# Four early expert tiles instead of two, three places for weights, and buffers of their own for the experts' squares

## The chip, the cores and the metric

One NeuronCore of one Trainium2 chip runs the whole program; the other cores are idle. The metric is the device time of one execution in microseconds. Beside it a profile gives, for one execution, every instruction's start and duration on the engines TensorE (PE, its weight loads as PEld), VectorE (DVE), ScalarE (ACT), GpSimd (POOL) and the queue engine SyncE (SP), and the clock that TensorE was granted.

## The reference

Three layers stand in a chain. Each token comes out of the first as one row of 512 numbers (8 heads of 64); there are 4 x 768 = 3072 tokens.

```python
# 1. retention: a decaying state per batch element and head
state = gamma * state + einsum('bhd,bhe->bhde', k[:, :, t], v[:, :, t])
y[:, :, t] = scale * einsum('bhd,bhde->bhe', q[:, :, t], state)
# 2. dense layer with a leaky activation: 512 -> 2048 -> 512
h = x @ w_in
x2 = (maximum(h, 0) + alpha * minimum(h, 0)) @ w_out
# 3. eight experts, each token goes to the one with the largest logit
expert_idx = argmax(normed(x2) @ normed(expert_emb).T / tau, axis=1)
out[mask] = gate_w[mask, None] * (maximum(x2[mask] @ w1[e], 0) @ w2[e])   # 512 -> 1024 -> 512
```

## The kernel before, in words

**Precision.** Every large product is taken in fp16 with both operands split into a high and a low half: high x high, high x low and low x high, three matmuls for one, summed in PSUM.

**Blocks.** The 3072 tokens are 24 tiles of 128, in 6 blocks of 4 tiles. For each block the retention makes the rows, and the dense layer runs as 16 steps: `mm1` gives 128 of the 2048 hidden columns for all 512 tokens of the block (12 matmuls with 512 columns), ScalarE and VectorE apply the activation and split the result, and `mm2` (four tiles of 3 matmuls) adds them into four accumulators. Of the last block the four tiles' `mm2` run with delays of 0, 2, 4 and 5 steps, so that its tiles end one after the other.

**Routing.** When a tile's accumulator is full, `Route` squares it, splits it into a payload of 514 words (512 values as two fp16 halves, gate weight, token number), transposes the payload by DMA on the SP queue, multiplies it with the experts' embeddings, takes the largest logit, and finds the row in a DRAM table where the token goes: expert e owns rows 3072 e and on, in the order of arrival. POOL scatters the payload there by an indirect DMA. Blocks 0 to 4 are routed a block at a time; the last block tile by tile, since everything behind it waits for it.

**The experts' weights.** From the second block on (about 200 to 650 us) the 8 experts' weights are split to fp16 halves and written to the DRAM buffer `wsplit`, in 16 halves of four pieces. `half_scale` (L729) squares the four raw pieces on ScalarE, for the sum that sets the scale; the squares themselves are thrown away, into a corner of one of the output buffers (`out_ring.bufs[g % 2]`). TensorE adds the sums over the partitions (`total`). Then `half_pair` (L739) splits each piece into the next of the two output buffers of `out_ring` (ScalarE writes the high half, VectorE the low half), SP writes it to `wsplit` (512 KB) and loads a further raw piece. Raw pieces and output buffers are parts of one 32 KB buffer per partition, `stage`.

**Experts' tiles.** A tile is 128 rows of the table of one expert: POOL gathers the rows by an indirect DMA, SP transposes them by DMA, `mm1e` (96 matmuls with 128 columns) and `mm2e` (24 matmuls with 512 columns) run on TensorE, VectorE scales the result, and POOL scatters it to the output. Which expert a tile belongs to is computed in the kernel: even tiles take the experts from the first up, odd tiles from the last down. Tile t's weights (`load_w`, four pieces of 1 MB, L1177) are fetched only where the expert changes, into `win16` for even tiles and `wout16` for odd ones, the places of the dense layer's weights, as these come free.

**Early tiles.** After block 4, `pick` (L851) takes the expert with the most tokens so far and gathers its first two tiles (t = -2 and -1), whose rows are in the table already. Their weights go to `stage`. These two tiles give TensorE work while the last block is routed. All other tiles (0 to 21 always, up to 7 more under a condition) follow when the counts of all tokens are known.

**Order.** The program is recorded and then ordered by a planner (`Plan.issue`, L252): it simulates engines and DMAs with fixed costs, takes at each step the instruction that can start first (a matmul only 1500 ns after what it waits for on another engine), and writes each engine's instructions in that order. On the chip each engine runs its own list strictly in order, and so does the SP queue. Since every instruction is recorded through one helper, nearly all rows of the trace carry its line, L146; a row is told apart by the buffers it names. Buffer names in the trace: `stage<-stage` on ScalarE is a square of `half_scale`, `stage<-stage,se` a split of `half_pair`; `wsplit<-stage` the write; `acce` the sums; `hat_buf` the early tiles' columns, `qk_buf` their payloads; `f_buf` in the experts' part the gathered payloads; `xT` there the columns and results.

Of the kernel before, what the change touches and what calls it, by code (L numbers as in the profile page):

```python
# [26 lines left out]
BW = BT * P  # L27
KD = DM // P
KF = DFF // P
NPRE = 2  # L30
NMIN = NTILE - NPRE
NSLOT = NMIN + E - 1
SL = 30
# [14 lines left out]
_n = 0  # L48
for _name, _w in (
    ("ks", NCH * H), ("w8", E), ("base8", E), ("first", E * E),  # L50
    ("tau0", SL), ("odd", SL), ("tidx", SL), ("p", 1), ("prow", NPRE), ("ones", P), ("tok", NTILE),
):
    _COLS[_name] = (_n, _n + _w)
    _n += _w
# [3 lines left out]
def _constants():  # L58
    gamma = 1.0 - 2.0 ** (-5.0 - np.arange(H))
    p = np.arange(P)  # L60
    c32 = np.zeros((P, NCOL), np.float64)

    def put(name, a):
        lo, hi = _COLS[name]
        c32[:, lo:hi] = np.broadcast_to(np.asarray(a, np.float64).reshape(-1, hi - lo), (P, hi - lo))

    c = np.arange(NCH)
    put("ks", gamma[None, None, :] ** -(P * c[None, :, None] + p[:, None, None] + 1.0))
    e = np.arange(E)
# [8 lines left out]
    put("prow", E * CAP + P * np.arange(NPRE)[None, :] + p[:, None])  # L78
# [247 lines left out]
def retention_prelu_moe_kernel(ctx: ExitStack, tc, qkv, w_in, w_out, alpha, emb, tau, w1, w2,  # L326
# [14 lines left out]
    def buf(name, shape, dt=F32):  # L341
        return sbuf.tile([P, *shape], dt, name=name, tag=name)
# [102 lines left out]
    def square_sum(src, acc, junk):  # L445
        A.activation(out=junk, in_=src, func=AF.Square, accum_out=acc)
# [268 lines left out]
    iwe = [buf(f"iwe{g}", [E]) for g in range(2)]  # L715
    HALVES = [(e, which) for e in range(E - 1, -1, -1) for which in range(2)]
    raw_ring = Ring([stage[:, 2 * k:2 * k + 2, :].rearrange("p c x -> p (c x)") for k in range(6)])
    out_ring = Ring([stage16[:, 2 * k:2 * k + 2] for k in (6, 7)])
    half_t = {}

    def half_load(p):
# [7 lines left out]
    def half_scale(n):  # L729
        e, which = HALVES[n]  # L730
        acc = tmp("acce", [4])
        for g in range(4):
            square_sum(half_t[n, g], acc[:, g:g + 1], out_ring.bufs[g % 2][:, :, 0, :])
        s = tmp("se", [1])
        c = (C_W1, C_WIDE)[which]
        pow2_inverse(pow2(total(acc, 4), s, c), iwe[which][:, e:e + 1], c)
        half_t[n] = s
# [108 lines left out]
    sel, m8 = buf("sel", [E]), buf("m8", [1])  # L846
    pre_idx = buf("pre_idx", [2], I32)
    pre_e = buf("pre_e", [1], I32)
    pre_row, first_row, first_other = buf("pre_row", [1]), buf("first_row", [1]), buf("first_other", [1])

    def pick():  # L851
        ps = m_ring.next()
        T.matmul(out=ps[:, 0:E], lhsT=ones16, rhs=csum, start=True, stop=True)
        m = tmp("pm", [1], n=1)
        V.tensor_reduce(out=m, in_=ps[:, 0:E], axis=AX.X, op=ALU.max)
        w = tmp("pw", [E], n=1)
        V.scalar_tensor_tensor(out=w, in0=ps[:, 0:E], scalar=m, in1=col("w8"), op0=ALU.is_equal, op1=ALU.mult)
        V.tensor_reduce(out=m8, in_=w, axis=AX.X, op=ALU.max)
        V.tensor_scalar(out=sel, in0=w, scalar1=m8, scalar2=None, op0=ALU.is_equal)
        V.tensor_scalar(out=pre_e, in0=m8, scalar1=-1.0, scalar2=float(E), op0=ALU.mult, op1=ALU.add)  # L860
        row = tmp("prow", [1], n=1)
        V.tensor_scalar(out=row, in0=m8, scalar1=-float(CAP), scalar2=None, op0=ALU.mult)
        V.tensor_scalar(out=pre_idx, in0=col("prow"), scalar1=row, scalar2=None, op0=ALU.add)
        V.tensor_tensor(out=pre_row, in0=col("prow")[:, 0:1], in1=row, op=ALU.add)
        V.scalar_tensor_tensor(out=first_row, in0=sel[:, 0:1], scalar=float(NPRE * P), in1=col("p"),
                               op0=ALU.mult, op1=ALU.add)
        V.tensor_tensor(out=first_other, in0=pre_row, in1=first_row, op=ALU.subtract)

# [38 lines left out]


    PRE = range(-NPRE, 0)
    wbuf = (win16, wout16, stage16)  # L910

    def cutter(buf_):
        words, at_ = buf_, [0]
# [23 lines left out]
        return [Ring([view(cut(n)) for _ in range(k)]) for view, n, k in parts]  # L937

    PAY, XT, H2 = (as_pay, PW), (as_xt, 512), (as_h2, 1024)
    pre_pay, = carve(qk_buf, (*PAY, NPRE))  # L940
    pre_xt, = carve(hat_buf, (*XT, NPRE))
    pre_h2, = carve(vp_buf, (*H2, NPRE))
    gather_ring, = carve(f64_buf, (*PAY, 6))
    xt_ring, = carve(xT[NB % 2], (*XT, 3))
    y_ring, = carve(xT[(NB - 1) % 2], (lambda a: a, DM, 4))
    h2_ring = Ring(carve(st_bd, (*H2, 2))[0].bufs + carve(x2T_buf, (*H2, 1))[0].bufs)
    opt_xt, opt_pay = carve(stage, (*XT, NSLOT - NMIN), (*PAY, NSLOT - NMIN))
    gt, x2T, h2, slot_idx = {}, {}, {}, []

    def gather(t):  # L950
# [126 lines left out]
    def sl(shape, dt=F32):  # L1077
# [3 lines left out]
        if dt != F32:  # L1081
# [17 lines left out]

    ntl = sl([E])  # L1100
    V.tensor_scalar(out=ntl, in0=ci, scalar1=1, scalar2=None, op0=ALU.max)
    V.scalar_tensor_tensor(out=ntl, in0=sel, scalar=-float(NPRE), in1=ntl, op0=ALU.mult, op1=ALU.add)

    t8 = sl([E, E])
    V.tensor_tensor(out=t8, in0=col("first").rearrange("p (a b) -> p a b", a=E),
# [9 lines left out]
    prod = sl([SL, E - 1])  # L1115
    wts = sl([2, E - 1])
    dsel = sl([E - 1])
    V.tensor_tensor(out=dsel, in0=sel[:, 1:E], in1=sel[:, 0:E - 1], op=ALU.subtract)
    V.tensor_scalar(out=wts[:, 0, :], in0=ntl[:, 0:E - 1], scalar1=-float(P), scalar2=float(CAP),
                    op0=ALU.mult, op1=ALU.add)  # L1120
    V.scalar_tensor_tensor(out=wts[:, 0, :], in0=dsel, scalar=float(NPRE * P), in1=wts[:, 0, :], op0=ALU.mult, op1=ALU.add)
# [38 lines left out]

    iw12 = sl([E])
    V.tensor_tensor(out=iw12, in0=iwe[0], in1=iwe[1], op=ALU.mult)
    pre_w = buf("pre_w", [1])
    ew = sl([E])
    V.tensor_tensor(out=ew, in0=iw12, in1=sel, op=ALU.mult)
    V.tensor_reduce(out=pre_w, in_=ew, axis=AX.X, op=ALU.add)
    wsl = sl([SL])
    for e in range(E):
        eq = tmp("eq", [SL])
# [7 lines left out]
    def load_w(t):  # L1177

        for piece in range(4):
            which, o = divmod(piece, 2)  # L1180
            dst = wbuf[t % 2 if t >= 0 else 2][:, 4 * piece:4 * piece + 4].rearrange("p c a x -> p (c a x)")
# [5 lines left out]
            which_e = pre_e[0:1, 0:1] if t < 0 else ctl[0:1, 0, t:t + 1]  # L1187
# [12 lines left out]
    def mm1e(t):  # L1200
        xt = x2T.pop(t)
        w = wbuf[t % 2 if t >= 0 else 2]
        h = h2[t] = (pre_h2 if t < 0 else h2_ring).next()
        for q in range(2):
            ps = x_ring.next()
            with plan.unit("PE"):
# [14 lines left out]
    def mm2e(t):  # L1221
        h = h2.pop(t)
        g = gt.pop(t)
        w = wbuf[t % 2 if t >= 0 else 2]
        ps = h_ring.next()
        for q in range(2):
            with plan.unit("PE"):
# [5 lines left out]
        if t >= 0:  # L1233
# [2 lines left out]
                                   op0=ALU.mult, op1=ALU.add)  # L1236
        y = y_ring.next()
        V.tensor_scalar(out=y, in0=ps, scalar1=g.bitcast(F32)[:, DM:DM + 1],
                        scalar2=wsl[:, t:t + 1] if t >= 0 else pre_w, op0=ALU.mult, op1=ALU.mult)
# [93 lines left out]
```

## Time and profile before

| | before |
|---|---|
| median of three runs | 1017.08 us (1011.92 to 1018.13) |
| profiled execution | 1014.34 us, span 1012.6 us |
| TensorE busy | 929.1 us (92%) |
| VectorE busy | 569.1 us (56%) |
| ScalarE busy | 466.2 us (46%) |
| GpSimd busy | 93.3 us (9%) |
| mean granted clock of TensorE | 0.967 |

The span reaches from the first to the last instruction; the execution is a little longer. Busy TensorE time counts matmuls as if they had their full length, so that at the low clock it is busy for longer with the same work. A wait in the trace is the idle time of an engine just before an instruction, with what ended it.

### The profile page before, as it was taken

How to read it: one execution, taken by the hardware profiler on the slowest of the kernel's cores; microseconds unless marked ns; L12 is line 12 of the kernel's file. 1: busy time of each engine (PE TensorE's matmuls, PEld its weight loads, DVE VectorE, ACT ScalarE, POOL GpSimd, SP SyncE). 2: the span in 40 equal slices, each digit the busy share in tenths (PEclk: the TensorE clock that was granted, in tenths of full speed). 3: DMA queues.
4: the chain of work that ended last, by engine and by line, in shares of the span. 5: the costliest groups of instructions: out<-in, count | busy, mean ns of one | idle time of the engine just before them, and what ended most of it. 6: DMA issues, size and time to landing. Idle time of an engine off the chain costs nothing. (4 is left out here: it accounts for less than half of the span.)

```text
span 1012.6 us, 18929 instructions
## 1 busy us (share of the span) xinstructions
PE 929.1 (92%) x7100; PEld 558.5 (55%) x7100; DVE 569.1 (56%) x1477; ACT 466.2 (46%) x825; POOL 93.3 (9%) x110
## 2 busy tenths in 40 slices
PE   5797889999998999999999899999599999988995
PEld 5774555555544544444444344446476776765763
DVE  4889988488766866686556448638422221221231
ACT  2568865385767777686565557322011010110100
POOL 0000000000100020001000200111311211232010
PEclk9798879999999999999999999999799999999998
DMA  8988623547789866766676655687564599634760
GB/s 298 303 255 268 221 97 112 177 115 196 253 231 231 201 228 221 218 209 209 197 208 187 209 166 161 237 322 176 136 194 115 141 308 319 174 95 114 165 269 23
DMA packets 129823, 201.44 MB, mean 199 GB/s; under 512 B 89726, under 2 KB 90110, under 8 KB 124608
## 3 DMA queue, kind: packets, MB, share of 16 engines
q1 hardware_dynamic: 123168, 179.42, 59.8%
q0 software_dynamic: 6560, 20.77, 6.0%
q8 instruction: 57, 0.93, 0.4%
q14 instruction: 38, 0.31, 0.1%
HBM read 204.59 MB, written 51.14 MB: 253 GB/s over the span
## 5 line engine op out<-in xcount | busy, mean ns | idle before, releaser
L146 PE MATMUL bank<-xT,win 128*128 128x512 f16 (+1 forms) x2208 | 335.5, 308 | 19.9 <-DMA xT<-f_buf 9.4
L146 PEld LDWEIGHTS <-win 128*128 128x128 f16 x2400 | 186.0, 99 | 158.2 <-issue 30.8
L146 PE MATMUL bank<-wout,f_buf 128*128 128x512 f16 x960 | 223.2, 379 | 3.9 <-DVE pay_buf L146 2.8
L146 PEld LDWEIGHTS <-f_buf 128*128 128x128 f16 x960 | 92.2, 99 | 109.3 <-issue 5.8
L146 DVE SCALAR_TENSOR_TENSOR stage<-stage,se 128x1024 f16<-128x1024 f32 x64 | 81.4, 1284 | 40.8 <-ACT stage L146 36.2
L146 DVE SCALAR_TENSOR_TENSOR g<-g,oma,bank 128x512 f32<-128x512 f32 x96 | 71.0, 742 | 41.9 <-ACT g L146 41.5
L146 ACT ACTIVATE st_bd<-bank 128x512 f16<-128x512 f32 x30 | 17.9, 597 | 156.9 <-PE bank L146 121.0
L146 ACT ACTIVATE stage<-stage,se 128x1024 f16<-128x1024 f32 x64 | 71.8, 1142 | 34.1 <-DMA wsplit<-stage 30.9
L146 ACT ACTIVATE stage<-stage 128x1024 f16<-128x1024 f32 x64 | 67.4, 1054 | 34.9 <-DMA wsplit<-stage 30.4
L146 ACT ACTIVATE g<-bank 128x512 f32<-128x512 f32 x96 | 56.2, 588 | 52.5 <-PE bank L146 51.1
L146 DVE SCALAR_TENSOR_TENSOR f_buf<-g,f_buf 128x512 f16<-128x512 f32 x80 | 55.0, 687 | 38.7 <-ACT f_buf L146 37.0
L146 POOL DMA_INDIRECT table<-pay_buf,rposi x24 | 26.2, 1092 | 500.6 <-DVE csum L146 138.0
L146 PEld LDWEIGHTS <-wout 128*128 128x128 f16 x1152 | 65.5, 98 | 7.9 <-issue 5.0
L146 PE MATMUL bank<-xT,wout 128*128 128x128 f16 x1056 | 62.6, 219 | 3.7 <-issue 3.6
L146 ACT ACTIVATE f_buf<-g 128x512 f16<-128x512 f32 x80 | 49.8, 622 | 33.0 <-DVE g L146 32.9
L146 PEld LDWEIGHTS <-st_bd 128*128 128x128 f16 x408 | 39.7, 99 | 45.4 <-issue 1.9
L146 DVE SCALAR_TENSOR_TENSOR st_bd<-bank,st_bd 128x512 f16<-128x512 f32 x34 | 23.5, 690 | 67.1 <-ACT st_bd L146 67.0
L146 DVE TENSOR_SCALAR xT<-bank,f_buf,cqk_sb 128x512 f32<-128x512 f32 x22 | 17.8, 809 | 67.1 <-PE bank L146 67.0
L146 PE MATMUL bank<-win,st_bd 128*128 128x512 f16 x216 | 49.5, 387 | 0.0
L146 POOL DMA_INDIRECT out<-xT,ids x25 | 25.3, 1011 | 217.0 <-DVE xT L146 184.1
L146 PE MATMUL bank<-wout,stage 128*128 128x512 f16 (+1 forms) x200 | 44.6, 375 | 0.0
L146 PE MATMUL bank<-wout,st_bd 128*128 128x512 f16 x192 | 42.7, 379 | 0.0
(249 smaller groups left out, 1129.8 us busy)
## 6 DMA issues: line engine op xcount, KB each, us to landing
win<-wsplit SPq DMA_DIRECT2D x56, 1024.0 KB
wout<-wsplit SPq DMA_DIRECT2D x52, 1024.0 KB
stage<-in_w SPq DMA_DIRECT2D x64, 512.0 KB
wsplit<-stage SPq DMA_DIRECT2D x64, 512.0 KB
qk_buf<-in_qkv SPq DMA_DIRECT2D x15, 768.0 KB
f_buf<-in_w_in SPq DMA_DIRECT2D x12, 512.0 KB
vp_buf<-in_qkv SPq DMA_DIRECT2D x20, 256.0 KB
f_buf<-in_w_out SPq DMA_DIRECT2D x10, 512.0 KB
```

What stands on the lines that cost most here:

```text
L146: call = lambda: fn(**kw)
```

## The change

The first two early tiles keep their places (t = -4 and -3, weights in `stage`). A second pair (t = -2 and -1) is added: `pick` runs its choice twice. If the largest expert has at least 512 tokens so far, the second pair is its third and fourth tile; otherwise its count is put below all others and the second pair is the next largest expert's first two tiles. The second pair's weights go to `win16`. Main tiles take `wout16` (even) and `stage` (odd); the optional tiles' rows and columns, which lay in `stage`, lie in `win`. Main tiles are 0 to 19 and up to 7 optional ones. The index arithmetic behind the last block uses `taken`, the sum of the two choices, in place of `sel`.

For the split of the experts' weights, two spare chunks at the end of `win` and `wout` are used: the one as a third output buffer of `out_ring`, the other as two buffers for the thrown-away squares (`junk_ring`).

```diff
-NPRE = 2
+NPAIR = 2
+NPRE = 2 * NPAIR
...
-    out_ring = Ring([stage16[:, 2 * k:2 * k + 2] for k in (6, 7)])
+
+    tail = [w[:, KF:KF + 2].rearrange("p c x -> p (c x)").bitcast(F16) for w in (win, wout)]
+    out_ring = Ring([stage16[:, 2 * k:2 * k + 2] for k in (6, 7)] + [tail[0].rearrange("p (c a x) -> p c a x", c=2, a=2)])
+    junk_ring = Ring([tail[1][:, 1024 * k:1024 * k + 1024].rearrange("p (c x) -> p c x", c=2) for k in range(2)])
...
-            square_sum(half_t[n, g], acc[:, g:g + 1], out_ring.bufs[g % 2][:, :, 0, :])
+            square_sum(half_t[n, g], acc[:, g:g + 1], junk_ring.next())
...
+        count = tmp("pcnt", [E], n=1)
+        V.tensor_copy(out=count, in_=ps[:, 0:E])
+        for k in range(2):
+            m = tmp(f"pm{k}", [1], n=1)
+            V.tensor_reduce(out=m, in_=count, axis=AX.X, op=ALU.max)
+            w = tmp(f"pw{k}", [E], n=1)
+            V.scalar_tensor_tensor(out=w, in0=count, scalar=m, in1=col("w8"), op0=ALU.is_equal, op1=ALU.mult)
+            V.tensor_reduce(out=m8[k], in_=w, axis=AX.X, op=ALU.max)
+            V.tensor_scalar(out=sel[k], in0=w, scalar1=m8[k], scalar2=None, op0=ALU.is_equal)
+            V.tensor_scalar(out=pre_e[k], in0=m8[k], scalar1=-1.0, scalar2=float(E), op0=ALU.mult, op1=ALU.add)
+            row = tmp(f"prow{k}", [1], n=1)
+            V.tensor_scalar(out=row, in0=m8[k], scalar1=-float(CAP), scalar2=None, op0=ALU.mult)
+            if k == 0:
+                V.tensor_tensor(out=pre_row, in0=col("prow")[:, 0:1], in1=row, op=ALU.add)
+                again = tmp("pagain", [1], n=1)
+                V.tensor_scalar(out=again, in0=m, scalar1=float(NPRE * P), scalar2=None, op0=ALU.is_ge)
+                less = tmp("pless", [1], n=1)
+                V.tensor_scalar(out=less, in0=again, scalar1=float(2 * NT), scalar2=-float(2 * NT), op0=ALU.mult, op1=ALU.add)
+                V.scalar_tensor_tensor(out=count, in0=sel[0], scalar=less, in1=count, op0=ALU.mult, op1=ALU.add)
+            else:
+                V.scalar_tensor_tensor(out=row, in0=again, scalar=float(NPAIR * P), in1=row, op0=ALU.mult, op1=ALU.add)
+            V.tensor_scalar(out=pre_idx[:, NPAIR * k:NPAIR * k + NPAIR], in0=col("prow"), scalar1=row, scalar2=None, op0=ALU.add)
+        V.tensor_tensor(out=taken, in0=sel[0], in1=sel[1], op=ALU.add)
...
-    wbuf = (win16, wout16, stage16)
+
+    def wbuf(t):
+        return stage16 if t < -NPAIR else win16 if t < 0 else (wout16, stage16)[t % 2]
+
...
-    pre_pay, = carve(qk_buf, (*PAY, NPRE))
-    pre_xt, = carve(hat_buf, (*XT, NPRE))
-    pre_h2, = carve(vp_buf, (*H2, NPRE))
+    pre_pay = Ring(carve(qk_buf, (*PAY, NPAIR))[0].bufs + carve(buf("pay2", [NPAIR, PW]), (*PAY, NPAIR))[0].bufs)
+    pre_xt = Ring(carve(hat_buf, (*XT, NPAIR))[0].bufs + [as_xt(flat(p)) for p in p16])
+    pre_h2, = carve(vp_buf, (*H2, NPAIR))
...
-    opt_xt, opt_pay = carve(stage, (*XT, NSLOT - NMIN), (*PAY, NSLOT - NMIN))
+    opt_xt, opt_pay = carve(win, (*XT, NSLOT - NMIN), (*PAY, NSLOT - NMIN))
...
-    V.scalar_tensor_tensor(out=ntl, in0=sel, scalar=-float(NPRE), in1=ntl, op0=ALU.mult, op1=ALU.add)
+    V.scalar_tensor_tensor(out=ntl, in0=taken, scalar=-float(NPAIR), in1=ntl, op0=ALU.mult, op1=ALU.add)
...
-        h = h2[t] = (pre_h2 if t < 0 else h2_ring).next()
+        h = h2[t] = (pre_h2 if t < -NPAIR else h2_ring).next()
...
-    load_w(-1)
-    for t in PRE:
-        mm1e(t)
-    for t in PRE:
-        mm2e(t)
-    load_w(0)
+    for t in (-NPRE, -NPAIR, 0):
+        load_w(t)
+    for first_t in (-NPRE, -NPAIR):
+        for t in range(first_t, first_t + NPAIR):
+            mm1e(t)
+        for t in range(first_t, first_t + NPAIR):
+            mm2e(t)
     load_w(1)
```

## Rows read from the trace of the kernel before

**Rows 1.** Busy time by stretch: stretch, length, PE, PEld, DVE, ACT, POOL, clock, DMA, GB/s

```profile
300.00:400.00 100.00, 91.50 (x585) 47.12 (x584) 71.05 (x190) 72.37 (x137) 7.26 (x8) 1.00 0.77 223
400.00:500.00 100.00, 94.71 (x571) 46.90 (x571) 66.18 (x173) 68.60 (x127) 5.28 (x8) 1.00 0.71 217
500.00:600.00 100.00, 93.01 (x463) 42.18 (x462) 55.53 (x131) 60.61 (x102) 5.54 (x8) 0.97 0.67 200
...
652.00:690.00 38.00, 36.91 (x179) 16.72 (x178) 15.80 (x75) 9.56 (x18) 4.39 (x6) 1.00 0.90 312
...
700.00:720.00 20.00, 14.71 (x139) 8.88 (x137) 15.27 (x91) 1.98 (x6) 6.00 (x6) 0.95 0.33 75
```

**Rows 2.** TensorE's timeline, 709 to 743: start, length, instruction, count, [idle before, releaser]

```profile
709.37 5.34 PE L146 MATMUL bank<-stage,vp_buf 128*128 128x512 f16 x24
724.14 6.46 PE L146 MATMUL bank<-xT,win 128*128 128x128 f16 x76 [9.44 <-DMA xT<-f_buf]
731.60 1.28 PE L146 MATMUL bank<-xT,win 128*128 128x128 f16 x20 [1.00 <-issue]
732.71 5.52 PE L146 MATMUL bank<-xT,wout 128*128 128x128 f16 x96
738.07 5.34 PE L146 MATMUL bank<-win,st_bd 128*128 128x512 f16 x24
```

**Rows 3.** Busy time by stretch, around the first main tile

```profile
720.00:725.00 5.00, 0.86 (x9) 0.86 (x9) 0.22 (x1) 0.00 (x0) 0.63 (x2) 0.50 0.91 180
725.00:730.00 5.00, 5.00 (x65) 5.00 (x63) 0.00 (x0) 0.00 (x0) 3.78 (x5) 0.69 0.50 156
```

**Rows 4.** Timeline of the SP queue, 669 to 720

```profile
673.04 2.78 SPq L146 DMA_TRANSPOSE hat_buf<-qk_buf  x2
...
682.27 4.96 SPq L146 DMA_TRANSPOSE x2T_buf<-pay_buf  x2
...
719.26 1.25 SPq L146 DMA_TRANSPOSE xT<-f_buf  x1
```

**Rows 5.** Waits of TensorE, 150 to 690: total, times, longest

```profile
PE bank L146 <- ACT stage L146: 11.7, 10, 3.6
```

**Rows 6.** Waits of ScalarE, 200 to 690: total, times, longest

```profile
ACT stage L146 <- DMA wsplit<-stage: 61.3, 42, 3.9
```

**Rows 7.** Timeline of ScalarE, 555 to 578: a split and a square

```profile
566.74 1.15 ACT L146 ACTIVATE stage<-stage,se 128x1024 f16<-128x1024 f32 x1 [1.66 <-DMA wsplit<-stage]
...
576.61 1.06 ACT L146 ACTIVATE stage<-stage 128x1024 f16<-128x1024 f32 x1 [3.12 <-DMA wsplit<-stage]
```

**Rows 8.** Timeline of the SP queue, 563 to 580

```profile
569.67 0.45 SPq L146 DMA_DIRECT2D wsplit<-stage  x1
```

**Rows 9.** Timeline of TensorE, 569 to 585

```profile
570.07 2.75 PE L146 MATMUL bank<-xT,win 128*128 128x512 f16 x12
...
578.99 0.59 PE L146 MATMUL bank<-acce,cst 128*128 128x4 f32 x2 [3.57 <-ACT stage L146]
579.44 5.28 PE L146 MATMUL bank<-xT,win 128*128 128x512 f16 x12
```

**Rows 10.** The page's costliest groups: instruction, count, busy, mean ns, idle before, releaser

```profile
L146 POOL DMA_INDIRECT out<-xT,ids x25 | 25.3, 1011 | 217.0 <-DVE xT L146 184.1
```

**Rows 11.** Timeline of POOL, 669 to 735

```profile
669.49 1.06 POOL L146 DMA_INDIRECT qk_buf<-table,pre_idx  x1 [0.60 <-DVE f_buf L146]
...
724.41 1.00 POOL L146 DMA_INDIRECT out<-xT,qk_buf  x1 [4.37 <-DMA out<-xT,qk_buf]
...
729.69 1.00 POOL L146 DMA_INDIRECT f_buf<-table,cqk_sb  x1 [0.30 <-issue]
```

**Rows 12.** Timeline of VectorE at the choice of the expert

```profile
645.31 0.17 DVE L146 TENSOR_REDUCE pm<-bank 128x1 f32<-128x8 f32 x1 [0.51 <-PE bank L146]
```

**Rows 13.** Timeline of TensorE at the gathers of the optional tiles

```profile
902.78 4.56 PE L146 MATMUL bank<-xT,wout 128*128 128x128 f16 x76
...
912.95 6.77 PE L146 MATMUL bank<-win,st_bd 128*128 128x512 f16 x24
```

More of the change, by code (lines that the diff above doesn't have):

```diff
@@ L50 @@
     ("ks", NCH * H), ("w8", E), ("base8", E), ("first", E * E),
-    ("tau0", SL), ("odd", SL), ("tidx", SL), ("p", 1), ("prow", NPRE), ("ones", P), ("tok", NTILE),
+    ("tau0", SL), ("odd", SL), ("tidx", SL), ("p", 1), ("prow", NPAIR), ("ones", P), ("tok", NTILE),
 ):
@@ L77, in _constants @@
     put("p", p[:, None])
-    put("prow", E * CAP + P * np.arange(NPRE)[None, :] + p[:, None])
+    put("prow", E * CAP + P * np.arange(NPAIR)[None, :] + p[:, None])
     put("ones", np.ones(P))
@@ L843, in finish @@
                                      in_=self.pay[o], in_offset=None, bounds_check=E * CAP - 1, oob_is_err=False)
-    sel, m8 = buf("sel", [E]), buf("m8", [1])
-    pre_idx = buf("pre_idx", [2], I32)
-    pre_e = buf("pre_e", [1], I32)
+    sel, m8 = [buf(f"sel{k}", [E]) for k in range(2)], [buf(f"m8_{k}", [1]) for k in range(2)]
+    taken = buf("taken", [E])
+    pre_idx = buf("pre_idx", [NPRE], I32)
+    pre_e = [buf(f"pre_e{k}", [1], I32) for k in range(2)]
     pre_row, first_row, first_other = buf("pre_row", [1]), buf("first_row", [1]), buf("first_other", [1])
@@ L853, in pick @@
         T.matmul(out=ps[:, 0:E], lhsT=ones16, rhs=csum, start=True, stop=True)
[L854 to L865, printed above, removed]
+        count = tmp("pcnt", [E], n=1)
[20 more added lines that the diff above has]
+            V.tensor_scalar(out=pre_idx[:, NPAIR * k:NPAIR * k + NPAIR], in0=col("prow"), scalar1=row, scalar2=None, op0=ALU.add)
@@ L866, in pick @@
+        V.tensor_tensor(out=taken, in0=sel[0], in1=sel[1], op=ALU.add)
+        V.scalar_tensor_tensor(out=first_row, in0=taken[:, 0:1], scalar=float(NPAIR * P), in1=col("p"),
                                op0=ALU.mult, op1=ALU.add)
@@ L1117, in retention_prelu_moe_kernel @@
     dsel = sl([E - 1])
-    V.tensor_tensor(out=dsel, in0=sel[:, 1:E], in1=sel[:, 0:E - 1], op=ALU.subtract)
+    V.tensor_tensor(out=dsel, in0=taken[:, 1:E], in1=taken[:, 0:E - 1], op=ALU.subtract)
     V.tensor_scalar(out=wts[:, 0, :], in0=ntl[:, 0:E - 1], scalar1=-float(P), scalar2=float(CAP),
                     op0=ALU.mult, op1=ALU.add)
-    V.scalar_tensor_tensor(out=wts[:, 0, :], in0=dsel, scalar=float(NPRE * P), in1=wts[:, 0, :], op0=ALU.mult, op1=ALU.add)
+    V.scalar_tensor_tensor(out=wts[:, 0, :], in0=dsel, scalar=float(NPAIR * P), in1=wts[:, 0, :], op0=ALU.mult, op1=ALU.add)
     V.tensor_tensor(out=wts[:, 1, :], in0=cnt[:, 1:E], in1=cnt[:, 0:E - 1], op=ALU.subtract)
@@ L1162, in retention_prelu_moe_kernel @@
     V.tensor_tensor(out=iw12, in0=iwe[0], in1=iwe[1], op=ALU.mult)
[L1163 to L1166, printed above, removed]
+    pre_w = [buf(f"pre_w{k}", [1]) for k in range(2)]
+    for k in range(2):
+        ew = sl([E])
+        V.tensor_tensor(out=ew, in0=iw12, in1=sel[k], op=ALU.mult)
+        V.tensor_reduce(out=pre_w[k], in_=ew, axis=AX.X, op=ALU.add)
     wsl = sl([SL])
@@ L1180, in load_w @@
             which, o = divmod(piece, 2)
-            dst = wbuf[t % 2 if t >= 0 else 2][:, 4 * piece:4 * piece + 4].rearrange("p c a x -> p (c a x)")
+            dst = wbuf(t)[:, 4 * piece:4 * piece + 4].rearrange("p c a x -> p (c a x)")
             cols = slice(4096 * o, 4096 * o + 4096)
@@ L1186, in load_w @@
                 continue
-            which_e = pre_e[0:1, 0:1] if t < 0 else ctl[0:1, 0, t:t + 1]
+            which_e = pre_e[t >= -NPAIR][0:1, 0:1] if t < 0 else ctl[0:1, 0, t:t + 1]
             def load(which=which, dst=dst, which_e=which_e, cols=cols):
@@ L1201, in mm1e @@
         xt = x2T.pop(t)
-        w = wbuf[t % 2 if t >= 0 else 2]
-        h = h2[t] = (pre_h2 if t < 0 else h2_ring).next()
+        w = wbuf(t)
+        h = h2[t] = (pre_h2 if t < -NPAIR else h2_ring).next()
         for q in range(2):
@@ L1223, in mm2e @@
         g = gt.pop(t)
-        w = wbuf[t % 2 if t >= 0 else 2]
+        w = wbuf(t)
         ps = h_ring.next()
@@ L1238, in mm2e @@
         V.tensor_scalar(out=y, in0=ps, scalar1=g.bitcast(F32)[:, DM:DM + 1],
-                        scalar2=wsl[:, t:t + 1] if t >= 0 else pre_w, op0=ALU.mult, op1=ALU.mult)
+                        scalar2=wsl[:, t:t + 1] if t >= 0 else pre_w[t >= -NPAIR], op0=ALU.mult, op1=ALU.mult)
         G.indirect_dma_start(out=out, out_offset=bass.IndirectOffsetOnAxis(ap=ids, axis=0),
                              in_=y, in_offset=None, bounds_check=NT - 1, oob_is_err=False)
-    load_w(-1)
-    for t in PRE:
-        mm1e(t)
-    for t in PRE:
-        mm2e(t)
-    load_w(0)
+    for t in (-NPRE, -NPAIR, 0):
[5 more added lines that the diff above has]
+            mm2e(t)
     load_w(1)
```

## The prediction

> **What bounds the kernel now.** I read the table of stages first: TensorE is busy 91.50, 94.71 and 93.01 us of the three 100 us stretches between 300 and 600, 36.91 of the 38 us from 652 to 690, and only 14.71 of 20 us from 700 to 720 [rows 1]. So it is bound by TensorE, and only its idle time can be won. That idle time lies in two places that this change touches.
>
> The first is the turn from the dense layers to the experts. In TensorE's timeline [rows 2] the two early tiles end with the 24 matmuls at 709.37 (5.34 us, so at 714.71); the next tile's first matmul starts at 724.14, after 9.44 us of idleness, released by the transpose of its gathered rows. That tile is also slow: it fills 724.14 to 732.71 = 8.57 us where the next tile's same 96 matmuls fill 732.71 to 738.07 = 5.36. Of the 3.21 us of difference, 1.00 is a pause with no named releaser [rows 2]; the rest goes with the granted clock, 0.50 from 720 to 725 and 0.69 from 725 to 730, the lower of two levels (1.2 GHz) for part of it [rows 3]. The turn costs 9.44 + 3.21 = 12.65 us. What sets its length is the routing of the last block: the transpose of tile 0's rows leaves SP only at 719.26 [rows 4], and the columns are there at 724.14.
>
> The second is the stretch in which the experts' weights are split, 200 to 650. TensorE waits ten times for ScalarE's squares, 11.7 us in all, 3.6 at most [rows 5]. ScalarE itself waits 42 times, 61.3 us, for a write to DRAM to leave a staging buffer [rows 6]. One instance shows why. A pair's split starts at 566.74, after a wait of its own of 1.66 us [rows 7]; its write is issued at 569.67 [rows 8]; the square that wants the same buffer for its unused output starts at 576.61, having waited 3.12 us [rows 7]. The buffer was held about 9.8 us, 6.9 of them after the issue. TensorE's sum over the squares then starts at 578.99 after 3.57 us of idleness, and the next 12 matmuls take 5.28 us where the group at 570.07 took 2.75 [rows 9]: 2.53 us more behind that gap. So the second place costs 11.7 + 2.53 = 14.2 us.
>
> **The change, part by part.** *Four early tiles.* No tile is added: the profile counts 25 scatters of main tiles beside the 2 early ones [rows 10], 27 in all, and afterwards it is 23 and 4. (Counting the reference's own routing on its inputs with seed 0 gives 5, 1, 5, 5, 5, 2, 3 and 1 tiles, also 27; there one expert already has 525 tokens before the last block, over 512, so both pairs are its own.) What moves is 2 x (5.36 + 5.34) = 21.4 us of TensorE work [rows 2], from the end of the loop to before the first main tile. TensorE then has work until about 714.7 + 21.4 = 736.1, while the columns of tile 0 came at 724.14: the gap is covered with 12.0 us to spare. The clock's part of the slow tile should go with the gap. The 1.00 us pause I leave in: it comes right behind five indirect transfers in a row on POOL, from 724.41 to 729.69 [rows 11], and such a run stays. That leaves 12.65 - 1.00 = 11.65 us won.
>
> What pays for it: two more gathers on POOL, 1.06 us each, spaced 1.37, and two more transposes on SP (2.78 us for two) [rows 4, 11]. The present pair is gathered from 669.49 on and SP starts to transpose at 673.04, 3.55 us later. The third and fourth gather would leave at about 672.2 and 673.6, land at 675.8 and 677.2, and leave SP free at 678.6. Three weight pieces stand behind them on SP, 0.45 us each as the issue in [rows 8], 1.4 us; the next thing that matters there, the first transpose of the last block, starts at 682.27 [rows 4]. So some 2 us remain and I price it at nothing; were that cover gone, the last block's routing would come up to 3 us later, which the 12.0 us to spare take up. The choice of the second expert puts 13 small operations on VectorE and two more for its scale, near 0.17 us each as the row of the present choice [rows 12]: 2.6 us, most of it at about 645, with the early tiles beginning only at about 714.7 - 21.4 = 693. POOL has four early scatters instead of two, each able to hold what is behind it until the one before has landed (4.37 us at 724.41 [rows 11]), against 10.7 us per tile: nothing.
>
> *Three weight places.* The second pair's weights go where tile 0's went, so the loads by 690 are the same bytes; tile 1's 4 MB go to the third place once the first pair is done at 714.7, against a need at about 747. SP may stand behind that wait, but its next transpose is that of 719.26 [rows 4]. The DMA engines, 0.90 busy from 652 to 690, are at 0.33 from 700 to 720 [rows 1]. Nothing. The optional tiles' buffers move to a place that is free by then: nothing.
>
> *Own buffers for the squares and a third output buffer.* No instruction is added. The squares no longer wait for any write. The splits come back to a buffer after three pairs, not two; pairs are about 6 us apart near 566.74, so some 18 us against a hold of 9.8: nothing should wait there. From below this is worth nothing or a little less than nothing (TensorE's order is written out in advance and shifts). From above it is 14.2 us, plus the other waits in the same stretch that follow late ScalarE work. I take two thirds of 14.2, 9.5 us, an estimate: it is nearer the upper end because the row at 576.61 shows the wait passing on to TensorE at nearly its full length (3.12 of 3.57), and not at the end because ScalarE keeps its own queue of work.
>
> Against that part stands a rule. In the Trainium skill's "DMA: Bandwidth & Descriptors", section "Anatomy of one DMA", a transfer costs about 2.0 us plus its bytes at 436 GB/s (fitted on the POOL queue; these are SP's), which for 512 KB would be an estimate of 3.2 us; buffers would then hardly ever be late, and the sum would be the turn's 11.65 us alone. The rows disagree: 6.9 us from issue to release [rows 7, 8].
>
> **Sum.** 11.65 + 9.5 = 21.2 us off. The profiled execution took 1014.34 us (span 1012.6), so 993.1; the median of the three runs shown, 1017.08, is 2.7 higher, and 21.2 off that is 995.9. I say **995**.
>
> **Rivals.** *Only the turn wins* (0.22). TensorE's waits in the middle stay because ScalarE, not the write, is late for another reason. For it: the squares are issued among other ScalarE work in a fixed order. Against: the write is late, and TensorE with it [rows 7, 9]. Time: 1017.08 - 11.65 = 1005.4; with a stall like the one at the gathers of the optional tiles, where 96 matmuls took from 902.78 to 912.95, 10.17 us instead of 5.36 [rows 13], moved into the turn, 1009. The rule of the Trainium skill above points to this case.
>
> *The middle wins all* (0.08). Every wait there goes, also those for VectorE that follow late ScalarE work. The idle time from 300 to 600 is 8.50 + 5.29 + 6.99 = 20.8 us [rows 1]; with the turn 32.4: 984, and less if the clock adds to it.
>
> *The order runs ahead of ScalarE* (0.07 slower, 0.13 level). The planner no longer sees a write before the squares, so it may place TensorE's 16 sums over them earlier than ScalarE gets there, and TensorE stops in order. Price: each such stop can cost 3.57 + 2.53 us [rows 9]. The 16 sums cost 14.2 now. If each cost 2.5 us, 40 in all, the change would be 40 - 14.2 - 11.65 = 14.2 us slower, 1031. It decides from 1.62 us a sum, where the turn's gain is used up (16 x 1.62 = 25.9); over 1% slower from 2.3. Against it: ScalarE's work per sum does not grow and it loses 61.3 us of waits.
>
> **How the numbers follow.** About 1% is what a measurement of this kernel can tell from no change, 1006.9 to 1027.3. The forecast, with its own range 986 to 1001, has 0.50; the turn alone 0.22, three quarters of it below 1006.9; all of the middle 0.08; level 0.13; slower 0.07. So faster 0.50 + 0.08 + 0.165, near 0.74, level 0.19, slower 0.07. The range 982 to 1010 holds the forecast, the turn alone, half of the larger win and a little of the level case.
>
> **What would show it.** Right: no idle time of TensorE above 2 us from 690 to 740, clock 1.00 there, 96 + 96 matmuls of the second pair between 714 and 736; ScalarE's waits for the writes of the split weights under 15 us and TensorE's waits for ScalarE's squares under 5. Wrong: a new wait of TensorE in front of a logits product between 687 and 704 (the SP queue was too full); VectorE or ScalarE as releaser in front of the sums in the middle; TensorE pauses of several us at a burst of gathers between 715 and 740.

## The result, and the profile after

The changed kernel takes 985.50 us (median of four runs, 983.46 to 988.65); the kernel before took 1016.94 us beside it (four runs, 1011.92 to 1018.13). The ratio is 0.9708, with a 95% interval from 0.9665 to 0.9752: 25 to 34 us faster. The forecast was 995, a gain of 21.2 us, with a range from 982 to 1010. So the direction is right and the time lies in the range, near its lower end, but the gain is larger than forecast. The profiled executions, 1014.34 and 988.65 us, differ by 25.7 (that of the changed kernel is the slowest of its four runs); in what follows these two are compared, since only they have durations.

To see where the 25.7 us come from I cut both spans at three places which both kernels have: the first logits product (at 229.14 us before, 230.18 after), the start of the last block's run of 63 matmuls (673.59 and 650.25), and the start of the first early pair's last 24 matmuls (709.37 and 694.50); the last cut is the start of the last tile's 24 matmuls (996.00 and 970.30). The table of stages then has three rows: the splitting of the weights, the end of the dense layers, the experts. Columns are as in [rows 1]. First the kernel before:

```profile
229.14:673.59 444.45, 422.17 (x2463) 206.99 (x2461) 290.21 (x761) 287.46 (x522) 31.61 (x42) 0.99 0.70 214
673.59:709.37 35.78, 34.69 (x344) 22.05 (x343) 24.99 (x180) 10.46 (x26) 3.00 (x3) 1.00 0.80 213
709.37:996.00 286.63, 270.29 (x3002) 195.41 (x3001) 68.82 (x157) 26.27 (x44) 56.89 (x56) 0.98 0.63 180
```

Then the changed kernel, and below the three rows 15 us out of its middle row, to be used later:

```profile
230.18:650.25 420.07, 416.24 (x2460) 207.07 (x2459) 291.82 (x775) 283.09 (x517) 31.91 (x44) 1.00 0.74 226
650.25:694.50 44.25, 36.92 (x344) 22.53 (x343) 25.36 (x180) 10.58 (x26) 2.99 (x3) 0.92 0.91 228
694.50:970.30 275.80, 269.46 (x3003) 194.57 (x3002) 68.02 (x155) 26.28 (x44) 54.73 (x54) 0.98 0.64 178
...
660.00:665.00 5.00, 4.01 (x19) 1.61 (x17) 4.02 (x34) 0.89 (x3) 0.00 (x0) 1.00 1.00 416
665.00:670.00 5.00, 0.04 (x1) 0.05 (x2) 0.00 (x0) 0.00 (x0) 0.00 (x0) 0.75 1.25 127
670.00:675.00 5.00, 5.00 (x21) 1.96 (x22) 3.23 (x29) 1.77 (x5) 0.00 (x0) 0.56 0.51 139
```

TensorE does the same work in each row (2463 and 2460 matmuls, 344 and 344, 3002 and 3003; some records are missing), so length is what changed:

| stretch | before | after | difference | of it idle | of it busy |
|---|---|---|---|---|---|
| splitting of the weights | 444.45 | 420.07 | -24.38 | -18.45 | -5.93 |
| end of the dense layers | 35.78 | 44.25 | +8.47 | +6.24 | +2.23 |
| experts | 286.63 | 275.80 | -10.83 | -10.00 | -0.83 |

Their sum is -26.74; the stretch ahead of the first cut is 1.04 longer. Idle is length less busy time; busy time that falls with the same work is matmuls at a higher clock (granted 0.99 and 1.00 in the first row).

**First row.** In the kernel before, the list of TensorE's waits from 150 to 690 us (total, times, longest) goes on behind the 11.7 us of [rows 5] with waits for VectorE:

```profile
PE bank L146 <- DVE pay_buf L146: 2.8, 2, 2.4
PE bank L146 <- DVE rhb L146: 2.7, 2, 1.5
```

In the changed kernel the list holds nothing for ScalarE's squares any more, and less for VectorE:

```profile
PE bank L147 <- DMA x2T_buf<-pay_buf: 7.3, 2, 6.0
PE bank L147 <- DVE roh L147: 2.8, 1, 2.8
```

And ScalarE, 180 to 690. The square is now `wout<-stage`, as its unused output lies in the spare chunk of `wout`; the split is still `stage<-stage` for two buffers of three:

```profile
ACT wout L147 <- DMA stage<-in_w: 37.0, 32, 3.6
...
ACT stage L147 <- DMA wsplit<-stage: 5.7, 4, 2.0
```

The 61.3 us of [rows 6] have become 5.7 (and 2.1 for the third buffer). The squares wait now for the raw weights to be loaded, 37.0 us, but no wait of TensorE in this stretch is named after ScalarE.

**Second and third row.** TensorE's timeline from the last block on, as [rows 2] had it:

```profile
650.25 13.76 PE L147 MATMUL bank<-wout,f_buf 128*128 128x512 f16 x63
669.96 0.38 PE L147 MATMUL bank<-emb,x2T_buf 128*128 128x16 f16 x8 [5.95 <-DMA x2T_buf<-pay_buf]
670.20 5.44 PE L147 MATMUL bank<-wout,f_buf 128*128 128x512 f16 x15
...
694.50 5.34 PE L147 MATMUL bank<-stage,vp_buf 128*128 128x512 f16 x24
699.67 10.88 PE L147 MATMUL bank<-p,win 128*128 128x128 f16 x192
...
712.40 10.10 PE L147 MATMUL bank<-win,st_bd 128*128 128x512 f16 x46 [1.41 <-DVE st_bd L147]
722.34 2.85 PE L147 MATMUL bank<-xT,wout 128*128 128x128 f16 x47
```

The two rows of the kernel before that stand against the second and the third of these:

```profile
688.44 0.35 PE L146 MATMUL bank<-emb,x2T_buf 128*128 128x16 f16 x8 [1.09 <-DMA x2T_buf<-pay_buf]
688.65 3.40 PE L146 MATMUL bank<-wout,f_buf 128*128 128x512 f16 x15
```

At the turn nothing is left of the 9.44 us: the second pair (`p`, x192, 10.88 us for two tiles) follows the first, and the first main tile (`xT`, 722.34) follows the second pair. But there is a new wait, 5.95 us in front of the first logits product of the last block, where the kernel before waited 1.09 us; and the 15 matmuls behind it take 5.44 us instead of 3.40, with the granted clock at 0.56 from 670 to 675, near the lower of its two levels (1.2 GHz), after an almost idle stretch of 5 us. That is the second row of the table.

SP's timeline in that stretch:

```profile
649.02 3.52 SPq L147 DMA_TRANSPOSE p<-pay  x2
652.63 0.53 SPq L147 DMA_DIRECT2D wout<-wsplit  x1
654.32 1.51 SPq L1218 DMA_DIRECT2D win<-wsplit  x2
655.93 0.39 SPq L147 DMA_DIRECT2D wout<-wsplit  x1
658.93 8.89 SPq L147 DMA_TRANSPOSE x2T_buf<-pay_buf  x2
```

The transposes that the logits product needs leave SP 8.68 us after the run of 63 began (658.93 - 650.25). In the kernel before it is the same 8.68 (682.27 in [rows 4], less 673.59). So SP was not late. The columns, though, came 11.0 us after the issue (669.96), not 6.2 (688.44 before): while the transposes were under way, from 660 to 665, the DMA engines were full with 416 GB/s. What stands in front of them differs. The kernel before issues three weight pieces of 1 MB there, the last by 677.39, 4.9 us ahead of the transposes:

```profile
675.91 1.01 SPq L146 DMA_DIRECT2D win<-wsplit  x2
677.01 0.38 SPq L146 DMA_DIRECT2D wout<-wsplit  x1
```

The changed kernel issues four, the last by 656.32, 2.6 us ahead of them.

### The profile page after: what moved, and what is told of

Read it like the earlier page. It is cut to its first block, busy times and chain, and to the rows that moved or that the text cites. A ratio compares the mean times of both kernels' runs of the same rounds, so it can differ in the third digit from the quotient of the medians.

```text
span 986.9 us, 18868 instructions
## 1 busy us (share of the span) xinstructions
PE 926.3 (94%) x7100; PEld 558.7 (57%) x7100; DVE 571.3 (58%) x1490; ACT 464.6 (47%) x825; POOL 91.4 (9%) x110
## 5 line engine op out<-in xcount | busy, mean ns | idle before, releaser
L147 PE MATMUL bank<-xT,win 128*128 128x512 f16 x1152 | 270.7, 386 | 7.0 <-DVE g L147 7.0
L147 PEld LDWEIGHTS <-win 128*128 128x128 f16 x1344 | 123.3, 100 | 136.9 <-issue 15.7
L147 PEld LDWEIGHTS <-stage 128*128 128x128 f16 x1440 | 89.3, 98 | 26.8 <-issue 4.2
L147 ACT ACTIVATE wout<-stage 128x1024 f16<-128x1024 f32 x64 | 67.3, 1052 | 39.2 <-DMA stage<-in_w 38.6
L147 DVE SCALAR_TENSOR_TENSOR f_buf<-g,f_buf 128x512 f16<-128x512 f32 x80 | 55.1, 689 | 32.9 <-ACT f_buf L147 32.4
L147 DVE SCALAR_TENSOR_TENSOR stage<-stage,se 128x1024 f16<-128x1024 f32 x43 | 55.0, 1280 | 8.4 <-ACT stage L147 8.4
L147 PE MATMUL bank<-xT,stage 128*128 128x128 f16 x960 | 56.8, 220 | 3.2 <-issue 3.2
L147 PE MATMUL bank<-xT,wout 128*128 128x128 f16 x960 | 56.5, 220 | 1.8 <-issue 1.8
L147 ACT ACTIVATE stage<-stage,se 128x1024 f16<-128x1024 f32 x43 | 48.8, 1139 | 9.6 <-DMA wsplit<-stage 5.7
L147 PEld LDWEIGHTS <-x2T_buf 128*128 128x128 f16 x384 | 26.9, 99 | 34.1 <-DMA x2T_buf<-pay_buf 8.0
```

The costliest lines, as they stand in the source:

```text
L147: call = lambda: fn(**kw)
```

## Experiments

These runs are from three chips, each with the kernel before beside it. Times are compared on one chip; where runs of two chips are compared, it is by their ratio to the kernel before or by their rows.

**Each part alone** (these four on one chip; the kernel before takes 999.19 us there). *e1_buffers_only* is the kernel before with both kinds of new buffers and two early tiles:

```diff
-    out_ring = Ring([stage16[:, 2 * k:2 * k + 2] for k in (6, 7)])
+    tail = [w[:, KF:KF + 2].rearrange("p c x -> p (c x)").bitcast(F16) for w in (win, wout)]
+    out_ring = Ring([stage16[:, 2 * k:2 * k + 2] for k in (6, 7)] + [tail[0].rearrange("p (c a x) -> p c a x", c=2, a=2)])
+    junk_ring = Ring([tail[1][:, 1024 * k:1024 * k + 1024].rearrange("p (c x) -> p c x", c=2) for k in range(2)])
...
-            square_sum(half_t[n, g], acc[:, g:g + 1], out_ring.bufs[g % 2][:, :, 0, :])
+            square_sum(half_t[n, g], acc[:, g:g + 1], junk_ring.next())
```

> The kernel before with the third output buffer and the squares' own buffers, and still two early tiles. Theory A (the buffers' gain and the early tiles' gain are separate, and the buffers took away the 23.7 us between 241 us and the last block's run of matmuls): 1017 - 23.7 = 993, TensorE waiting under 2 us for ScalarE's squares, and no wait over 2 us of TensorE for the transpose of the last block's payload. Rival B (part of the middle's gain is the planner's new order, which the early tiles' loads and the moved buffers also shaped): 1000 or more.

Measured: 976.06 us, ratio 0.9788 [0.9755, 0.9821], a gain of 23.1 us. TensorE waits for no square, and the turn's gap is still there (7.51 us on this chip, for `xT<-f_buf`). The buffers alone are worth far more than the 9.5 us of the forecast.

*e2_early_only* is the other part alone: the changed kernel with the two old output buffers and the squares in them.

```diff
...
-    out_ring = Ring([stage16[:, 2 * k:2 * k + 2] for k in (6, 7)] + [tail[0].rearrange("p (c a x) -> p c a x", c=2, a=2)])
...
+    out_ring = Ring([stage16[:, 2 * k:2 * k + 2] for k in (6, 7)])
...
-            square_sum(half_t[n, g], acc[:, g:g + 1], junk_ring.next())
+            square_sum(half_t[n, g], acc[:, g:g + 1], out_ring.bufs[g % 2][:, :, 0, :])
```

> The changed kernel with the old two output buffers and the squares thrown into them: only the early tiles and the three weight places. Theory A: the turn wins 10.8 us and loses 8.5 in front of it, where TensorE waits for the transpose of the last block's payload (5.95 us and the low clock behind it), so 1017 - 2.3 = 1014 to 1015, with that wait present. Rival B (the wait in front of the turn comes from the buffers' part, since the middle now ends earlier and pushes writes and loads together): no such wait, 1017 - 11 = 1006.

Measured: 992.71 us, ratio 0.9935 [0.9909, 0.9961], a gain of 6.5 us, between the 2.3 of the theory and the 11 of the rival. The new wait is in it too, so it belongs to the early tiles:

```profile
690.32 0.38 PE L147 MATMUL bank<-emb,x2T_buf 128*128 128x16 f16 x8 [4.80 <-DMA x2T_buf<-pay_buf]
```

*e3_squares_only* has the squares' own buffers without the third output buffer, *e4_third_only* the third output buffer with the squares in the old corner. Both have two early tiles; the edits are the lines of e1 with `junk_ring` and the line with `out_ring`.

> The kernel before with the squares' own buffers alone; two output buffers. Theory A (it was the squares that waited for the writes, and TensorE's sums for the squares): most of the 23.7 us, 17 or more: 997 to 1000; ScalarE's waits for the writes of split weights fall from 61 to about 31 us, all of them before splits. Rival C (the splits' waits push all later ScalarE work, so the third output buffer is what counts): 1008 or more.

> The kernel before with a third output buffer alone; the squares are still thrown into the first two. Theory A: 3 to 8 us, 1009 to 1014, with most waits of TensorE for ScalarE's squares still there. Rival C: 15 us or more, 1002 or less.

Measured: e3 975.05 us, ratio 0.978 [0.9747, 0.9814]; e4 984.3 us, ratio 0.988 [0.984, 0.992]. The squares' buffers alone give all that both give: in e3 ScalarE still waits 14.5 us for writes (below), but no wait of TensorE is named after it, and e3 is as fast as e1.

```profile
ACT stage L146 <- DMA wsplit<-stage: 14.5, 13, 2.1
```

My expectation for e4 was too low: the third buffer alone brings 14.9 us, though 48.8 us of ScalarE's waits for writes and 7.1 us of TensorE's waits for squares remain. Both kinds of buffer treat the same wait, so their gains don't add.

**The removed wait, or a new order?** With other buffers the planner also writes another order. *e8_old_order* takes the squares out of the output buffers and tells the planner that they still write there, so each engine's list is as before. Its buffers are those of e3; the rest of the edit:

```diff
...
-            square_sum(half_t[n, g], acc[:, g:g + 1], out_ring.bufs[g % 2][:, :, 0, :])
+            src, a, junk = half_t[n, g], acc[:, g:g + 1], junk_ring.next()
+            old = out_ring.bufs[g % 2][:, :, 0, :]
+            plan.add("ACT", lambda src=src, a=a, junk=junk: nc.scalar.activation(out=junk, in_=src, func=AF.Square, accum_out=a),
+                     [src], [old, a], 95.0 + 0.833 * 1024 + 93.0)
```

> The kernel before with the squares written to their own buffers as in the run with the squares alone, but every engine's list of instructions left word for word in the order of the kernel before (the planner is told of the old buffer). Theory A (the removed waits themselves give the gain): within 3 us of the run with the squares alone, a ratio of 0.981 or less. Rival F (the planner's new order gives it, since it no longer sees the write before the squares): half of the gain or less, a ratio of 0.989 or more.

Measured: 991.08 us against 1011.47 of the kernel before on that chip, ratio 0.9805 [0.9774, 0.9835]. From the first logits product to the run of 63 it takes 420.47 us, as the changed kernel does:

```profile
230.57:651.04 420.47, 415.87 (x2462) 206.76 (x2461) 290.27 (x761) 287.43 (x522) 30.81 (x42) 1.00 0.73 226
```

So the gain of the first row is the wait itself; the new order adds nothing that these runs can tell (0.4 of 24.4 us between the two rows).

**The new wait in front of the logits product** (same chip as e8). *e5_changed_again* is the changed kernel, for comparison; *e6_late_weights* puts part of the second pair's weights and tile 0's behind the first two tiles' transposes on SP, by a bias (ns) in the planner's order.

```diff
-    def load_w(t):
+    def load_w(t, later=(0.0, 0.0)):
...
+            plan.bias = later[which]
...
-    for t in (-NPRE, -NPAIR, 0):
-        load_w(t)
+    for t, later in ((-NPRE, (0.0, 0.0)), (-NPAIR, (0.0, 45000.0)), (0, (50000.0, 50000.0))):
+        load_w(t, later)
```

> The changed kernel itself, beside the kernel before on the chip of the next three runs. If the two parts add up (0.9788 and 0.9935): a ratio of 0.972; if they overlap: 0.979.

> The changed kernel with one move: the second half of the second early pair's weights and all of tile 0's weights are issued on SP behind the first two transposes of the last block's payload, not in front of them. Theory A (those 4 MB fill the DMA engines just as the transposes start, and TensorE's 5.95 us wait and the low clock behind it come from that): the wait falls to 1.5 us or less and the kernel is 5 to 8 us faster than the changed one, a ratio near 0.965. Rival D (the two added transposes and gathers are what is in the way, on SP or POOL): the wait stays above 4 us and the time stays within 2 us of the changed kernel.

Measured: e5 985.67 us (980.65 to 988.00), ratio 0.9735 [0.9696, 0.9774]; e6 979.86 us (978.88 to 980.91), ratio 0.9691 [0.966, 0.9723]. In e6 SP issues the same transposes 8.68 us after the run of 63 (649.65), as ever, but with no weights in front of them, and with weights in front of the next two:

```profile
658.33 4.51 SPq L147 DMA_TRANSPOSE x2T_buf<-pay_buf  x2
664.24 1.54 SPq L1219 DMA_DIRECT2D win<-wsplit  x2
665.83 0.43 SPq L147 DMA_DIRECT2D wout<-wsplit  x1
667.69 9.04 SPq L147 DMA_TRANSPOSE x2T_buf<-pay_buf  x2
```

TensorE follows: there is no wait at the first product, and one of 2.55 us at the product that needs the second pair of transposes.

```profile
663.24 0.34 PE L147 MATMUL bank<-emb,x2T_buf 128*128 128x16 f16 x8
...
678.43 0.36 PE L147 MATMUL bank<-emb,x2T_buf 128*128 128x16 f16 x8 [2.55 <-DMA x2T_buf<-pay_buf]
```

Where the weights go, the wait goes. It is the megabytes in the DMA engines just ahead of the transposes that make the columns late, not a later issue from SP. The 5.8 us between e5 and e6 are within the forecast; the ranges of the two just touch (980.65 and 980.91). The Trainium skill's "DMA: Bandwidth & Descriptors", section "Queues, rings and completion order", says that each DMA engine takes up the descriptors of one ring in order; these rows agree with that (4.51 us without loads in front, 9.04 with them).

**Pauses at the optional gathers** (same chip again). Near its end the changed kernel pauses during and right behind POOL's runs of three and more indirect transfers, as the kernel before does in the 96 matmuls of 10.17 us in [rows 13]. *e7_spread_gathers* issues the optional tiles' gathers one by one.

```diff
+            if t >= 6 and t % 2 == 0:
+                gather(NMIN + (t - 6) // 2)
...
-    for t in range(NMIN, NSLOT):
-        gather(t)
```

> The changed kernel with the seven gathers of the optional tiles issued one by one behind main tiles 6, 8, ... 18 in place of two runs at the end. Theory A (a run of gathers is what makes TensorE pause near 880 to 900 without a named releaser, some 9 us with the low clock behind it): the pauses are gone and the kernel is 7 to 9 us faster than the changed one. Rival E (the pauses come from the instruction stream of the conditional tiles that follow, or from weight loads): they stay, 0 to 2 us.

Measured: 982.49 us (979.40 to 984.82), ratio 0.9715 [0.9676, 0.9753]: 3.2 us under e5, whose runs overlap with it. The pauses moved: from 730 to 830 each of the five runs of a scatter and two gathers has two short ones at its end, 0.6 to 1.4 us together, and the list of waits has 4.5 us of them where e5 has 5.3. Spreading is no clear gain.

**Do the gains add?** *e9_early_late_weights* is e2 with the bias of e6; *e10_late_spread* is the changed kernel with the edits of e6 and e7 (a third chip, 998.31 us for the kernel before).

> The early tiles and the three weight places with the old two output buffers, and with the weights moved behind the first two transposes as in the run with late weights. Theory A (the early tiles are worth the 11.65 us that were forecast for the turn, less what is lost in front of it): the wait in front of the turn falls to about 1 to 2.5 us and the ratio, 0.9935 with the wait, falls to 0.987 to 0.989. Rival G (TensorE's idle time at the turn only moves to another place): 0.991 or more.

> The changed kernel with both moves, the late weights and the seven gathers spread over the main tiles. If the two gains add up (5.8 and 3.2 us against the changed kernel): a ratio of 0.964 to 0.967, faster than either kernel of the comparison. If they do not: 0.969 or more.

Measured: e9 988.78 us, ratio 0.9907 [0.9879, 0.9936], which leaves theory and rival open: the wait in front of the first product is gone, but one of 3.14 us stands at a later one. e10 973.32 us, ratio 0.9749 [0.9696, 0.9802], against the theory; the changed kernel itself takes 972.10 us on that chip (e11, below), so the two moves won nothing there. On that chip TensorE shows none of the pauses, so there was nothing for e7's edit to win; and e10 has a wait of 3.83 us in front of a logits product and 2.0 and 0.6 us for weights that now come late.

*e11_changed_third* and *e12_buffers_again* are the changed kernel and e1 side by side on that chip (998.07 us for the kernel before).

> The changed kernel again, beside the buffers alone, on one chip. My theory: the early tiles give back in front of the first logits product (8.5 us in the changed kernel) most of what they win at the turn (10.8 us), so the changed kernel is only 0 to 4 us under the buffers alone. Rival: the two parts add as the runs of each alone do (0.9935 and 0.9788), and the changed kernel is 6 us or more under the buffers alone. A second rival: on a chip where the turn's gap is shorter (7.5 us instead of 9.4) the early tiles cost more than they win, and the buffers alone are the faster.

> Own buffers for the squares and the third output buffer, with two early tiles as before. My theory: 22 to 25 us under the kernel before on this chip, TensorE without waits in the middle, the turn's gap present (7 to 9 us, with a slow first tile behind it), and no wait above 1.5 us in front of a logits product. Rival: the middle wins less on this chip (under 18 us), and the missing part of the changed kernel's gain is the early tiles'.

Measured: e11 972.10 us (968.99 to 973.76), ratio 0.9722 [0.967, 0.9775]; e12 974.42 us (973.57 to 975.33), ratio 0.9755 [0.9708, 0.9802]. The medians differ by 2.3 us, within the 0 to 4 us of the theory, and the two ranges touch; so the early tiles are worth little here, if anything. The stages, cut at the same places, say why; first e12, with five us out of its middle row below:

```profile
228.88:647.93 419.05, 415.87 (x2460) 206.86 (x2459) 290.48 (x760) 283.92 (x517) 30.59 (x42) 1.00 0.73 227
647.93:682.44 34.51, 34.51 (x343) 22.12 (x342) 25.04 (x180) 10.46 (x26) 3.00 (x3) 1.00 0.72 221
682.44:955.83 273.39, 265.64 (x3002) 194.69 (x3001) 69.38 (x157) 26.27 (x44) 56.79 (x56) 0.99 0.67 188
...
655.00:660.00 5.00, 5.00 (x24) 2.25 (x23) 4.62 (x36) 2.06 (x4) 0.00 (x0) 1.00 0.68 185
```

Then e11, likewise:

```profile
227.36:646.56 419.20, 416.15 (x2459) 207.17 (x2458) 291.45 (x775) 283.23 (x517) 33.76 (x44) 1.00 0.73 227
646.56:690.21 43.65, 37.52 (x343) 22.71 (x342) 25.28 (x180) 10.57 (x26) 2.99 (x3) 0.92 0.86 229
690.21:954.85 264.64, 263.84 (x3002) 192.53 (x3001) 68.11 (x155) 26.27 (x44) 54.60 (x54) 1.00 0.66 186
...
655.00:660.00 5.00, 5.00 (x25) 2.23 (x23) 4.57 (x38) 1.38 (x3) 0.00 (x0) 1.00 1.00 408
```

The middle is equal (419.05 and 419.20). Behind the early pair e11 wins 8.75 us, in front of it it loses 9.14; in these two executions the early tiles' gain is spent in full. (The span of e11 is still 1.0 us shorter, because it reaches the first cut 1.5 us earlier, long before any early tile.) SP's timelines show how, first that of e12:

```profile
644.51 0.52 SPq L146 DMA_DIRECT2D wout<-wsplit  x1
645.13 3.32 SPq L146 DMA_DIRECT2D win<-wsplit  x2
...
656.61 4.47 SPq L146 DMA_TRANSPOSE x2T_buf<-pay_buf  x2
```

Then that of e11:

```profile
644.90 3.32 SPq L147 DMA_TRANSPOSE p<-pay  x2
648.31 0.53 SPq L147 DMA_DIRECT2D wout<-wsplit  x1
649.95 1.52 SPq L1218 DMA_DIRECT2D win<-wsplit  x2
651.57 0.38 SPq L147 DMA_DIRECT2D wout<-wsplit  x1
655.24 8.26 SPq L147 DMA_TRANSPOSE x2T_buf<-pay_buf  x2
```

In both the logits' transposes leave 8.68 us after the run of 63. In e12 the first of four weight pieces leaves 3.4 us ahead of that run, in e11 1.75 us behind its start, since the two added transposes (`p<-pay`, 3.32 us) stand before it. Four pieces are 4 MB, by estimate about 10 us at the 408 GB/s of e11's row or the 431 that e12 moves from 650 to 655. In e12 they are done when the transposes come (185 GB/s from 655 to 660), in e11 they are not (408 GB/s there): 8.26 us for the pair instead of 4.47, and TensorE waits 5.16 us.

## Why the prediction was right or wrong

**Four early tiles: right at the turn.** The step was 11.65 us; the third row of the table measures 10.83, and the gap of 9.44 is gone. The rest is made up otherwise than forecast: busy time fell by 0.83 and not by the 2.21 of the slow first tile, a new wait of 1.41 for VectorE came, and the pauses without a named releaser, which were to stay, fell from 6.7 to 4.9 us (from 640 on). Less the 8.47 lost in front of the turn, 2.4 us are left of the early tiles.

**"Own buffers" was mis-sized.** The step "I take two thirds of 14.2, 9.5 us" failed: it measured 24.38. Two things were left out. First, the 11.7 in it was only what the list names after ScalarE's squares. All idle time of TensorE in that stretch was 22.28 us, the rest under other names (VectorE's `pay_buf` 2.8, `rhb` 2.7, `nt` 1.3 and smaller ones), and 18.45 of it went: the list names the engine that stands last in a chain, here VectorE behind a late ScalarE. That these hang on the one wait is shown by e8, which removes it and keeps the order: there the idle time is 4.6 us (420.47 - 415.87). Second, 2.53 us was one slow group behind one gap; over the stretch the clock gave back 5.93. The cut to two thirds rested on ScalarE's own queue of work, after which neither the changed kernel's list of TensorE's waits nor that of e3 names any.

**"Nothing" for the weight places and the added transposes failed.** It was +8.47 us. The prediction named the place, "a new wait of TensorE in front of a logits product", but gave "the SP queue was too full" as the reason. SP's list held: 8.68 or 8.69 us in all of these kernels but e2 (9.77). The failed step is "three weight pieces stand behind them on SP, 0.45 us each": it priced a piece by its issue. By estimate a 1 MB piece holds the DMA engines for some 2.5 us at the 416 GB/s of the row from 660 to 665; there are four of them, and the columns come behind them. The 12.0 us to spare at the turn did not take this up, because TensorE itself stood still in front of the early tiles.

**The sum.** -9.5 - 11.65 was forecast; -24.38 - 10.83 + 8.47 came. The two misses have opposite signs, so 995 was nearer than its terms, and that is luck: without the 8.47 the same base would give 1017.08 - 35.21 = 981.9, just outside the range.

**The rivals.** "Only the turn wins" fell with e1 and e3. The Trainium skill's rule on one DMA ("DMA: Bandwidth & Descriptors", "Anatomy of one DMA"), by which a buffer of 512 KB would be held an estimated 3.2 us, spoke for it; the runs disagree, since taking the squares off these buffers gave 24.1 us (e3). "The order runs ahead of ScalarE" fell with the list of waits and with e8. "The middle wins all", given 0.08, was the right mechanism: its 32.4 us for the two places stand against 35.2 measured (24.38 + 10.83). The 8.47 lost between them is in no case of the prediction, so that its 984 lies so near to 985.50 is luck too. The 1009 given beside "Only the turn wins" does not come out of its own rows (1005.4 + 10.17 - 5.36 = 1010.2); nothing hangs on it.

**Signs.** ScalarE's waits for the writes, under 15, and TensorE's for squares, under 5, came as said. From 690 to 740 there is no idle time above 2 us and the clock is 1.00, as said too. But the times given were those of the kernel before, and the changed kernel is there some 24 us earlier: the second pair's 192 matmuls run from 699.67 to 710.55, and the logits product that stood at 688 waits from 664 to 670. That wait is the first sign of being wrong, and it came.

**Open.** e2 alone gained 6.5 us, the same tiles beside the buffers 2.3 us on another chip; why they differ isn't settled. e6, at 979.86 us, has a lower median than both kernels on its chip (1011.47 and 985.67), but with the same late weights e10 is no faster than the changed kernel on another (973.32 and 972.10).

## What to carry to other kernels

Where one engine is late, count all idle time of the bounding engine in that stretch and not only what is named after the late one; then take the single wait away with the order kept, to see how much hangs on it. Price a load by how long its bytes hold the DMA engines, not by its issue, and look which small urgent transfer stands right behind it. A thrown-away output needs a place, and a place that a DMA reads makes its writer wait (61.3 us of ScalarE here).

## What the runs showed of the hardware

The changed kernel has nine pauses of TensorE with no named releaser, 4.9 us in all from 640 on. They come during and right behind a run of POOL's indirect transfers (here six from 876.84 to 884.43), all among matmuls with 128 columns. The matmuls behind them are slower (7.23 us for 24, against 5.34), with the granted clock at 0.73 from 885 to 893:

```profile
885.42 0.37 PE L147 MATMUL bank<-xT,stage 128*128 128x128 f16 x2 [0.84 <-issue]
885.58 7.23 PE L147 MATMUL bank<-wout,st_bd 128*128 128x512 f16 x24
```

On a chip where the kernel before takes 998 us the same program (e11) runs through its gathers with no pause, and the 24 matmuls take 5.34 us again:

```profile
870.53 5.52 PE L147 MATMUL bank<-xT,stage 128*128 128x128 f16 x96
875.89 5.34 PE L147 MATMUL bank<-wout,st_bd 128*128 128x512 f16 x24
```

So the stretch of the experts takes 275.80 us on the one and 264.64 on the other with the same instructions, 11.2 of the 15.5 us between the two spans (986.9 and 971.4). All four runs on the chip of e5 to e8 have such pauses, and none of the eight on the other two chips has, so they go with the chip and not with the change. Nor does every run of transfers bring them: behind the changed kernel's seven from 714.20 to 723.11 there is none. Why they come on some chips only stays open.
